# Two edits of the DMA order in a four-layer attention kernel: halves for the late query loads, later stores of x

## The chip, the cores and the metric

The kernel runs on one core of one Trainium2 chip. The metric is the device time of one execution in microseconds (us), taken as the median of several runs. Times inside the kernel come from one execution recorded by the hardware profiler; they count from the first instruction of the program (the span's start).

## The reference

Four layers of attention, one after the other; layers 0 and 2 use weights A, layers 1 and 3 weights B. Each has 32 query heads of 16 dimensions, and a single key head and value head for all of them. The sequence has 2048 rows of 512 numbers, in 32-bit floating point.

```python
def _A_ref(x, wq, wk, wv, wo):          # _B_ref is the same
    B, S, D = x.shape                   # 1, 2048, 512
    H = 32
    Dh = D // H                         # 16
    q = (x @ wq).reshape(B, S, H, Dh).transpose(0, 2, 1, 3)
    k = x @ wk
    v = x @ wv
    scores = jnp.einsum("bhqd,bkd->bhqk", q, k) * (Dh ** -0.5)
    p = _softmax(scores, axis=-1)
    o = jnp.einsum("bhqk,bkd->bhqd", p, v)
    return o.transpose(0, 2, 1, 3).reshape(B, S, H * Dh) @ wo

x = A_x
x = x + _A_ref(_layernorm(x, axis=-1), A_wq, A_wk, A_wv, A_wo)
x = x + _B_ref(_layernorm(x, axis=-1), B_wq, B_wk, B_wv, B_wo)
x = x + _A_ref(_layernorm(x, axis=-1), A_wq, A_wk, A_wv, A_wo)
x = x + _B_ref(_layernorm(x, axis=-1), B_wq, B_wk, B_wv, B_wo)
```

There are 4 layers x 32 heads x 2048 x 2048 = 537 million scores, and each needs an exponential.

## The kernel before

**Units of work.** The queries of a layer come in 4 blocks `b` of 512 rows, and the heads in 4 groups `m` of 8. A pair (layer, block, group) is the unit whose queries are loaded together; there are 64 of them. A pair is worked off in halves: 64 keys by 4 of its 8 heads by 512 queries, which makes one tile of 128 x 1024 scores. A first matmul step (`score`, letter `S` in the order) writes such a tile `st` into PSUM, ScalarE (ACT) takes its exponential into one of 16 tiles `pt`, and TensorE (PE) multiplies `pt` with the values into `acc`. There are 4096 halves. 3658 of them take their exponential on ACT (line 868). The other 438 take it on VectorE (DVE), as a polynomial (lines 902 to 920): their scores go to the bank `by_v`, and `score_v` takes them `AHEAD` = 24 halves ahead of the one that `S` is at. Beside these run the products of the layer norm, keys, values, queries and outputs.

**What sets the order.** `ORDER` is a string of some 18,000 letters, worked out beforehand; each letter is one step on PE, ACT or DVE. The order of instructions on each compute engine is therefore fixed in the text. `Q` in that string calls `load_q`.

**Queries.** The queries of a pair are made on PE in 16 bits (`q_clamp`, `q_rest`), go out to a scratch tensor `qscr` (DMA `qs<-qs`, line 483), and come back by `load_q` in another layout as a tile `qt` of 128 partitions x 4 x 512 (512 KB, 4 KB a partition). The index of 4 counts two heads each: halves with `h` = 0 read `qt[:, 0:2]`, halves with `h` = 1 read `qt[:, 2:4]`. There are two `qt` buffers, so that a load can start when the scores of the pair before last have been made. Layer 0 goes over its first four pairs in four rounds of keys, and layers 1 to 3 over their first three pairs in two rounds, so that such a pair is loaded anew for each round: 85 loads in all.

**How a load is issued.** All these DMAs are issued by SyncE (SP), in program order on one queue; a DMA that has to wait holds up those behind it. `first_uses` works out from `ORDER` at which exponential each load is first used (`uses`). When that is `ROOM` = 20 or more exponentials away, `load_q` issues four quarters, three exponentials apart: the first at once, the others through the list `later`, which `issue_due` looks at after every exponential. `issue` makes such a DMA wait for the exponential before last:

```python
tc.add_manual_dep(d, exps[-2].name, ...)   # in issue(): exps[-1] is the one just written
```

59 loads go that way. When the first use is nearer, the whole 512 KB go as one DMA; that happens 26 times: 17 loads at the start of layer 0 (the first at 19.00 us, before the first exponential, the last at 232.80 us) and three each at 995 to 1025 us, 1841 to 1869 us and 2689 to 2716 us, where the next layer's first pairs begin. For the first the distance is 0, for the other 25 it is 5 to 7 exponentials, and in 21 of these the first reader is a `score_v` with `h` = 1.

**Residual.** `out_add` adds the attention's output to a tile of x (128 rows), and stores it to the scratch tensor `xscr` (DMA `xs<-xt`, line 510, 256 KB). It is loaded back a layer later (`xt<-xs`, line 398). There are 48 such stores.

Of the kernel before, what the change touches and what calls it, by code (L numbers as in the profile page):

```python
# [25 lines left out]
BQ = S // NB  # L26
# [8 lines left out]
ROOM = 20  # L35
# [233 lines left out]
def fast_path(ctx, tc, x_in, weights, out, flag):  # L269
    nc = tc.nc  # L270
    PE, V, A, G, SP = nc.tensor, nc.vector, nc.scalar, nc.gpsimd, nc.sync
# [13 lines left out]
    def need(*key):  # L285
        assert key in done, key
# [34 lines left out]
    xscr = [scr.tile([P, D], F32, name=f"xs{t}") for t in range(NT)]  # L321
# [177 lines left out]
    def out_add(l, t, ps):  # L499
        x = xt[l, t]  # L500
        V.scalar_tensor_tensor(x, ps, 1 / VS / WS, x, ALU.mult, ALU.add)
        del xt[l, t]
        if (l, t) == (NL - 1, NT - 1):
            for h, eng in enumerate((SP, A)):
                h = slice(64 * h, 64 * h + 64)
                eng.dma_start(out[t * P:(t + 1) * P, :][h], x[h])
        elif l == NL - 1:
            SP.dma_start(out[t * P:(t + 1) * P, :], x)
        else:
            SP.dma_start(xscr[t], x)  # L510
            xt[l + 1, t] = x


# [149 lines left out]
    def add_outputs(l, b, after):  # L663
        for t in range(4 * b, 4 * b + 4):
            def prods(t=t):
                c = slice((t - 4 * b) * P, (t - 4 * b + 1) * P)
                ps = []
                for m in range(NM):
                    ps += three([p[:, c] for p in ot[l, b, m]], [p[:, m] for p in wt["wo", l]])
                return ps  # L670

            add_product(prods, after, ("o", l, b))
            work.add_dve("oa", lambda t=t: out_add(l, t, beside), key=("end",))
        work.add_dve("od", lambda: done.add(("o", l, b)), key=("od", l, b))
# [77 lines left out]
    for l in range(NL):  # L752
        first = 16 * l
        n, cuts = (4, [0, 4, 8, 12, NK]) if l == 0 else (3, [0, 12, NK])
# [19 lines left out]
    exps, later, loads = [], [], [0]  # L774

    def first_uses():

        n, v, some, count, open_ = 0, -1, set(), 0, False
        nth = [sum(k <= g for k in to_load) - 1 for g in range(len(groups))]
        uses = {}  # L780
        for what in ORDER:
            if what == "S":
                while n in some:
                    n += 1
                uses.setdefault(nth[halves[n][0]], count)
                n += 1
                count += 1
            for w in STEPS[what] if what in STEPS and what != "S" else "":
                if w in "VW":
                    if not open_:  # L790
                        while n in some:
                            n += 1
                        v = max(v + 1, n + (AHEAD if n < len(halves) - LATE else NEAR))
                        some.add(v)
                        uses.setdefault(nth[halves[v][0]], count)
                    open_ = not open_
        return uses

    uses = first_uses()
# [7 lines left out]
    def spaced(dmas, apart):  # L807

        for k, dma in enumerate(dmas):
            if k == 0 or apart == 0:  # L810
                dma()
            else:
                later.append((len(exps) + k * apart, dma))
        later.sort(key=lambda t: t[0])
# [6 lines left out]
    def load_q():  # L821
        g = to_load.popleft()
        l, b, m = pairs[groups[g][0]]
        need("q", l, b, m)
        t = qt[groups[g][0]] = qop.tile([P, 4, BQ], F16, name="qt")
        q = qscr[l % 2][b][m].rearrange("r t d h q -> (r t d) (h q)")
        k = loads[0]
        loads[0] += 1
        if uses[k] - len(exps) < ROOM:
            SP.dma_start(t, q.unsqueeze(1).to_broadcast([64, 2, 4 * BQ]))  # L830
            return

        def part(h):
            return SP.dma_start(t[:, h], q[:, h * BQ:(h + 1) * BQ].unsqueeze(1).to_broadcast([64, 2, BQ]))

        spaced([lambda h=h: part(h) for h in range(4)], 3)

    def moving(n, r):
        g, c, h = halves[n]
# [227 lines left out]
    def finish():  # L1067
# [43 lines left out]
        products(1, last)  # L1111
        products(3, first)
        out_add(l, 4 * b, banks[0])
        times(cs[2])
        invert(cs[3])
        rest(cs[2])
        products(2, last)
        out_add(l, 4 * b + 1, banks[1])
        times(cs[3])
        out_add(l, 4 * b + 2, banks[2])  # L1120
# [12 lines left out]
    with tc.manual_schedule():  # L1133
# [95 lines left out]
        for c in (0, 1):  # L1229
            part(c, others, scaled(stat[key, c]))  # L1230
        q_rest(0, 0, 0, ps, (SP, A))
        load_q()
        kps = st[1][:, 0:512]
        for c in range(NC):
# [24 lines left out]
    with tc.manual_schedule():  # L1259
        on_pe = [what for what in ORDER if what in STEPS or what in "FP"]  # L1260
        for what in ORDER:
            if what in on_pe[:1]:
                on_pe.pop(0)
            if what == "S":
                score()
            elif what in STEPS:
                step(what, on_pe[0] if on_pe else "S")
            elif what == "F":
                whole()
            elif what == "Y":  # L1270
                touch()
            elif what == "P":
                work.next_pe().whole()
            elif what == "X":
                work.step_dve()
            elif what == "I":
                exp_first()
            elif what in "01":
                chain("01".index(what))
            elif what == "G":  # L1280
                evacs.popleft()()
            elif what == "D":
                divs.popleft()()
            elif what == "Q":
                load_q()
            else:
                raise ValueError(what)
# [158 lines left out]
```

## Time and profile before

| | before |
|---|---|
| time, median of 3 runs | 3426.78 us (3426.61 to 3429.51) |
| the profiled execution's own time | 3429.39 us |
| its span, first to last instruction | 3427.6 us |
| TensorE clock granted | 0.999 |
| PE busy | 3360.2 us (98%), 97703 matmuls and as many weight loads |
| ACT busy | 3382.2 us (99%); the 3658 exponentials 3367.7 us |
| DVE busy | 3253.7 us (95%) |
| GpSimd busy | 134.1 us (4%) |
| DMA | 147.81 MB, 43 GB/s in the mean |

Three engines are busy nearly all the time, so the lost time is small and has to be looked for in single places: an idle stretch of ACT, what PE did then, and what the DMA queues moved. Exponentials overlap each other (one takes 1102 ns in the mean, and one starts every 925 ns), so that ACT shows as idle only after the previous one has ended. In the timeline a bracket such as [0.74 <-issue] means that the engine was idle for 0.74 us before the row and that nothing the profile shows ended the wait; SPq rows are DMA issues of SP, and `x2` merges two rows. In the table by stretches, the columns are the busy time of each engine with its number of instructions, the granted clock, the busy share of the 16 DMA engines and GB/s.

### The profile page before, as it was taken

The numbers are of one execution on the slowest core, as the hardware profiler recorded it, in microseconds if no ns is written. First come the engines' busy times: TensorE is split into PE (matmuls) and PEld (weight loads), VectorE is DVE, ScalarE is ACT, GpSimd is POOL, SyncE is SP. The second block draws the span as 40 slices with busy tenths as digits, with TensorE's granted clock in tenths as the row PEclk, the third lists the DMA queues.
The fourth block names the chain that finished last, engine by engine and source line by source line (L and its number), as shares of the span: only waits on it lengthen the run. The fifth ranks groups of instructions, "written<-read, shape, count | busy, mean of one in ns | idle before, by whom it ended". The sixth has DMA issues, their size and how long they took to land.

```text
span 3427.6 us, 206561 instructions
## 1 busy us (share of the span) xinstructions
PE 3360.2 (98%) x97703; PEld 2087.5 (61%) x97703; DVE 3253.7 (95%) x4436; ACT 3382.2 (99%) x3688; POOL 134.1 (4%) x137
## 2 busy tenths in 40 slices
PE   9999999999999999999999999999999999999998
PEld 5666566555566666646556666664646666554554
DVE  7889999999989999999998999999999899999998
ACT  8999999999999999999999999999999999999997
POOL 3000000000000000000000000000000000000000
PEclk9999999999999999999999999999999999999999
DMA  3121111011012111101012211110101211111010
GB/s 114 59 81 47 32 43 45 28 36 39 30 54 54 50 50 37 41 25 44 21 31 58 57 49 37 42 43 24 46 19 37 67 46 37 36 49 29 22 42 21
DMA packets 119316, 147.81 MB, mean 43 GB/s; under 512 B 32889, under 2 KB 81017, under 8 KB 118457
## 3 DMA queue, kind: packets, MB, share of 16 engines
q1 hardware_dynamic: 116888, 133.65, 13.5%
q8 instruction: 765, 12.53, 1.5%
q10 hardware_dynamic: 1568, 0.85, 0.1%
q14 instruction: 95, 0.77, 0.1%
HBM read 90.57 MB, written 34.59 MB: 37 GB/s over the span
## 4 chain that ended last, share of the span: by engine, by line
PE 62%; ACT 27%; DVE 8%; issue 2%; DMA 0%; DVEq 0%; ACTq 0%
PE acc L532 32%; ACT pt L868 27%; PE st L532 16%; PE beside L532 10%; PE by_v L532 2%; DVE pt L902 1%; DVE poly L919 1%; PE beside L426 1%; DVE pt L913 1%; DVE poly L920 1%; DVE mant L916 1%; DVE pt L918 1%; PE beside L569 0%; DVE sum L1017 0%; DVE vop L462 0%
## 5 line engine op out<-in xcount | busy, mean ns | idle before, releaser
L868 ACT ACTIVATE pt<-st 128x1024 f32<-128x1024 f32 x3658 | 3367.7, 1102 | 20.6 <-PE st L532 17.6
L532 PE MATMUL acc<-pt,vop 64*32 64x256 f32 (+1 forms) x51728 | 2893.8, 434 | 4.5 <-issue 2.1
L532 PE MATMUL st<-qt,kop 64*32 64x512 f16 x29264 | 1763.2, 380 | 48.7 <-ACT pt L868 25.1
L532 PEld LDWEIGHTS acc<-pt,vop 64*32 64x32 f32 x51728 | 1331.2, 106 | 253.5 <-DVE sum L1017 12.0
L532 PEld LDWEIGHTS <-kop 64*32 64x32 f16 x32768 | 797.2, 90 | 922.3 <-issue 642.6
L902 DVE TENSOR_SCALAR pt<-by_v 128x512 int32<-128x512 f32 x876 | 598.9, 684 | 36.2 <-PE by_v L532 31.1
L913 DVE SCALAR_TENSOR_TENSOR pt<-poly,pt 128x1024 f32<-128x1024 f32 x438 | 536.2, 1224 | 3.3
L920 DVE SCALAR_TENSOR_TENSOR poly<-poly,mant 128x1024 f32<-128x1024 f32 x438 | 535.6, 1224 | 3.1
L919 DVE SCALAR_TENSOR_TENSOR poly<-mant 128x1024 f32<-128x1024 f32 x438 | 534.5, 1221 | 0.0
L532 PE MATMUL beside<-xnT,wq 64*32 64x512 f16 x5760 | 438.8, 376 | 1.5 <-issue 0.6
L532 PE MATMUL beside<-wo,ot 64*32 64x512 f16 x5472 | 406.4, 376 | 0.5 <-DVE gqk L497 0.3
L532 PE MATMUL by_v<-qt,kop 64*32 64x512 f16 x3504 | 350.1, 376 | 1.8 <-DVE pt L902 1.3
L918 DVE TENSOR_SCALAR pt<-pt 128x1024 int32<-128x1024 int32 x438 | 304.8, 696 | 4.6
L916 DVE TENSOR_SCALAR mant<-pt 128x1024 int32<-128x1024 int32 x438 | 301.8, 690 | 6.3
L532 PEld LDWEIGHTS <-wq 64*32 64x32 f16 x5760 | 170.5, 92 | 49.7 <-issue 12.8
L532 PEld LDWEIGHTS <-ot 64*32 64x32 f16 x5472 | 158.6, 92 | 39.7 <-issue 4.9
L477 POOL TENSOR_TENSOR sq<-qs 128x512 bf16<-128x512 f16 x64 | 73.6, 1151 | 873.6 <-DVE qs L474 873.6
L532 PE MATMUL beside<-xnT,wkv 64*32 64x512 f16 x1344 | 97.5, 376 | 0.0
L1017 DVE COPY sum<-acc 128x512 f32<-128x512 f32 x126 | 84.1, 687 | 11.9 <-PE acc L532 8.3
L413 POOL TENSOR_TENSOR rstd<-var,nhalf 128x4 f32<-128x4 f32 x15 | 21.7, 1446 | 1451.0 <-DVE var L412 1451.0
L474 DVE TENSOR_SCALAR qs<-beside 128x512 f16<-128x512 f32 x62 | 42.7, 689 | 16.9 <-PE beside L532 9.5
L998 DVE COPY seen<-beside 128x1 f32<-128x1 f32 x92 | 14.3, 156 | 41.2 <-PE beside L532 34.2
(133 smaller groups left out, 833.5 us busy)
## 6 DMA issues: line engine op xcount, KB each, us to landing
qt<-qs SPq DMA_DIRECT2D x236, 128.0 KB
qs<-qs SPq DMA_DIRECT2D x127, 128.0 KB
rec<-rs SPq DMA_DIRECT2D x63, 256.0 KB
qt<-qs SPq DMA_DIRECT2D x26, 512.0 KB
xs<-xt SPq DMA_DIRECT2D x48, 256.0 KB
xt<-xs SPq DMA_DIRECT2D x48, 256.0 KB
sum<-sum SPq DMA_DIRECT2D x252, 32.0 KB
xt<-in_A_x_dram SPq DMA_DIRECT2D x30, 256.0 KB
```

The costliest lines, as they stand in the source:

```text
L426: PE.transpose(ps[:, c * P:(c + 1) * P], xn[:, c * P:(c + 1) * P], ident)
L474: V.tensor_scalar(qs[:, 0], ps, BIG, -BIG, ALU.min, ALU.max)
L477: G.tensor_tensor(sq, qs[:, 0], qs[:, 0], ALU.mult)
L532: PE.matmul(o[32 * j:32 * j + 32], w[j][h], x[j][h], start=start, stop=stop, skip_group_check=True, tile_position=(64 * r, 32 * j))
L868: e = A.activation(pts[:, i], st[s], AF.Exp, scale=SCALE / UP / UP).ins
L902: w = V.tensor_scalar(e[:, 512 * r:512 * r + 512], by_v, SCALE / UP / UP * LOG2E * 2.0 ** 23, LEAD, ALU.mult, ALU.add).ins
L913: writer[i] = V.scalar_tensor_tensor(p, poly, C0, p, ALU.add, ALU.mult).ins
L916: lambda: V.tensor_scalar(mant.bitcast(I32), e, 0x3FFFFF, 0x3F800000, ALU.bitwise_and, ALU.bitwise_or),
L918: lambda: V.tensor_scalar(e, e, 0x7FC00000, HALVES, ALU.bitwise_and, ALU.bitwise_or),
L919: lambda: V.scalar_tensor_tensor(poly, mant, C2, mant, ALU.add, ALU.mult),
L920: lambda: V.scalar_tensor_tensor(poly, poly, C1, mant, ALU.add, ALU.mult),
L1017: V.tensor_copy(sums[pr, odd], acc[odd])
```

## The change

The first edit is in `out_add`: the store of x isn't issued at once, but put on the list `later` with a due number two exponentials on. The second is in `load_q`: a near load goes as two DMAs of 256 KB (`n` = 2: heads' index 0:2 and 2:4, 2 KB a partition each) instead of one of 512 KB. The first half is issued at once. The second is put on `later` one exponential on (`apart` = 1), so that it waits for the end of the exponential that was written last before the load; for the first load (`k` = 0), `apart` is 0 and both halves are issued one after the other. The quarters of the far loads stay as they are.

```diff
@@ out_add
         else:
-            SP.dma_start(xscr[t], x)
+            later.append((len(exps) + 2, lambda: SP.dma_start(xscr[t], x)))
             xt[l + 1, t] = x
@@ load_q
-        if uses[k] - len(exps) < ROOM:
-            SP.dma_start(t, q.unsqueeze(1).to_broadcast([64, 2, 4 * BQ]))
-            return
+        n = 1 if uses[k] - len(exps) >= ROOM else 2
 
         def part(h):
-            return SP.dma_start(t[:, h], q[:, h * BQ:(h + 1) * BQ].unsqueeze(1).to_broadcast([64, 2, BQ]))
-
-        spaced([lambda h=h: part(h) for h in range(4)], 3)
+            return SP.dma_start(t[:, h:h + n],
+                                q[:, h * BQ:(h + n) * BQ].unsqueeze(1).to_broadcast([64, 2, n * BQ]))
+
+        spaced([lambda h=h: part(h) for h in range(0, 4, n)], 3 if n == 1 else k > 0)
```

The instructions of PE, ACT, DVE and GpSimd stand in the same order as before; only SP's queue changes. All query loads now have line 832, the stores keep 510, and lines further down are one less.

SP around the three loads at 995 to 1025 us, before (`qt<-qs` is a query load with partitions and elements, `qs<-qs` the store of new queries, `den`, `rs`, `sum` and `rec` the chain that divides by the softmax's sums):

```order
L483 DMA qs_1_0_141<-qs 64x2x512 x2
L830 DMA qt<-qs_0_1_138 128x1x2048
L830 DMA qt<-qs_0_2_139 128x1x2048
L483 DMA qs_1_1_142<-qs 64x2x512 x2
L1025 DMA den<-sum_22417 64x1x32
L1025 DMA den<-sum_22452 64x1x32
L483 DMA qs_1_2_143<-qs 64x2x512 x2
L830 DMA qt<-qs_0_3_140 128x1x2048
L1048 DMA rs_169<-den 4x16x32 x2
```

Each load was one DMA there, and the next rows of the queue stood right behind it. SP at the same place now:

```order
L483 DMA qs_1_0_141<-qs 64x2x512 x2
L832 DMA qt<-qs_0_1_138 128x1x1024 x2
L832 DMA qt<-qs_0_2_139 128x1x1024 x2
L483 DMA qs_1_1_142<-qs 64x2x512 x2
L1024 DMA den<-sum_22433 64x1x32
L1024 DMA den<-sum_22468 64x1x32
L483 DMA qs_1_2_143<-qs 64x2x512 x2
L832 DMA qt<-qs_0_3_140 128x1x1024 x2
L1047 DMA rs_169<-den 4x16x32 x2
```

Each is two DMAs of half the size; what stood behind a load now stands behind its second half, which waits for an exponential.

SP around a store of x that comes between quarters of a load (the one at 569.77 us), before:

```order
L510 DMA xs_158<-xt 128x512
L834 DMA qt<-qs_2_3_132 128x1x512 x3
L510 DMA xs_159<-xt 128x512
L834 DMA qt<-qs_2_3_132 128x1x512
L1025 DMA den<-sum_14323 64x1x32
L1025 DMA den<-sum_14343 64x1x32
L510 DMA xs_160<-xt 128x512
```

And now:

```order
L510 DMA xs_158<-xt 128x512
L832 DMA qt<-qs_2_3_132 128x1x512 x4
L1024 DMA den<-sum_14339 64x1x32
L1024 DMA den<-sum_14359 64x1x32
L510 DMA xs_159<-xt 128x512
L510 DMA xs_160<-xt 128x512
```

The middle store went behind the last quarter and two small DMAs. `later` is a queue in which a new entry stands behind what is there already, so a store that is put on it while quarters are waiting goes out only behind them. 8 of the 48 stores change their place in the queue; the other 40 keep it, and wait for an exponential there.

## The prediction

> **What bounds the kernel now.** I read the page first (busy shares, the groups), then ACT's idle time in stretches behind each kind of DMA that the change touches, then the timeline at the worst of these.
>
> ```profile
> PE 3360.2 (98%) x97703; PEld 2087.5 (61%) x97703; DVE 3253.7 (95%) x4436; ACT 3382.2 (99%) x3688; POOL 134.1 (4%) x137
> q8 instruction: 765, 12.53, 1.5%
> L868 ACT ACTIVATE pt<-st 128x1024 f32<-128x1024 f32 x3658 | 3367.7, 1102 | 20.6 <-PE st L532 17.6
> ```
>
> PE and ACT run in lockstep, both full. ACT's exponentials have only 20.6 us of idle time in all, and 17.6 us of that are waits for scores from PE. A change of DMAs alone, with every engine's order kept, can win little more than this, so the question is which of these 20.6 us lie behind the DMAs that change. I asked for the stretch from 3 to 10 us after each issue, for line 868 alone: 24 near loads (without the first two), 59 far loads (from their first quarter) and 48 stores of x.
>
> ```profile
> 998.60:1005.60 7.00, 6.07 (x8) 1.00 0.06 19
> 1011.67:1018.67 7.00, 7.00 (x9) 1.00 0.19 40
> 1027.53:1034.53 7.00, 6.18 (x7) 1.00 0.28 76
> 2718.87:2725.87 7.00, 5.97 (x8) 1.00 0.42 139
> ...
> sum 168.00, ACT 163.12; mean ACT 6.80
> sum 413.00, ACT 411.17; mean ACT 6.97
> sum 336.00, ACT 335.31; mean ACT 6.99
> ```
>
> The three sums are near loads, far loads, stores. Behind near loads ACT idles 168.00 - 163.12 = 4.88 us, or 0.20 us a load; behind far ones 1.83/59 = 0.03 us; behind stores 0.69/48 = 0.014 us. The rows above the sums show that near loads differ: the one at 1008.67 us cost nothing, the one at 995.60 us 0.93 us. So I looked at that one.
>
> ```profile
> 993.96 1.55 SPq L483 DMA_DIRECT2D qs<-qs  x2
> 995.60 0.56 SPq L830 DMA_DIRECT2D qt<-qs  x1
> 1001.51 0.40 PE L532 MATMUL acc<-pt,vop 64*32 64x256 f32 x2 [0.74 <-issue]
> 1002.39 1.02 ACT L868 ACTIVATE pt<-st 128x1024 f32<-128x1024 f32 x1 [0.88 <-PE st L532]
> q1 hardware_dynamic: 431, 0.79, 77.8%
> q8 instruction: 1, 0.02, 5.7%
> ```
>
> PE stood still for 0.74 us and waited for no semaphore ("issue"), long after the load's data had come. The last two rows are the DMA view of 995.20 to 999.15 us and of 999.15 to 1000.20 us. In the first there is only data, on 77.8% of the engines' time; in the second, once the data has drained, one packet of queue 8, of instructions. The page counts 765 such packets; 97703 + 97703 instructions of PE over 765 make 255 each. So I read queue 8 as PE's own program, 256 instructions a packet, at one packet every 3427.6/765 = 4.5 us. My reading: the fetch was asked for while 128 KB + 128 KB + 512 KB were on the way, came only when they had drained, and PE ran out of instructions. The same sign, ACT idle for scores some 6 to 8 us after a near load, stands at eight other places:
>
> ```profile
> 113.86 1.02 ACT L868 ACTIVATE pt<-st 128x1024 f32<-128x1024 f32 x1 [0.31 <-PE st L532]
> 154.99 1.94 ACT L868 ACTIVATE pt<-st 128x1024 f32<-128x1024 f32 x2 [0.36 <-PE st L532]
> 184.15 1.02 ACT L868 ACTIVATE pt<-st 128x1024 f32<-128x1024 f32 x1 [0.41 <-PE st L532]
> 1031.89 1.02 ACT L868 ACTIVATE pt<-st 128x1024 f32<-128x1024 f32 x1 [0.82 <-PE by_v L532]
> 1875.88 1.02 ACT L868 ACTIVATE pt<-st 128x1024 f32<-128x1024 f32 x1 [0.33 <-PE st L532]
> 2696.02 1.97 ACT L868 ACTIVATE pt<-st 128x1024 f32<-128x1024 f32 x2 [0.22 <-PE st L532]
> 2709.51 1.03 ACT L868 ACTIVATE pt<-st 128x1024 f32<-128x1024 f32 x1 [0.31 <-PE st L532]
> 2722.35 0.39 PE L532 MATMUL st<-qt,kop 64*32 64x512 f16 x3 [0.90 <-issue]
> 2722.79 1.02 ACT L868 ACTIVATE pt<-st 128x1024 f32<-128x1024 f32 x1 [1.03 <-PE st L532]
> ```
>
> These follow the loads at 106.87, 148.73, 177.07, 1024.53, 1868.73, 2689.00, 2701.63 and 2715.87 us; with the one at 995.60 us there are nine.
>
> **The change, part by part.**
>
> *Near loads, the stalls that can go.* The gain is bounded above by near loads behaving as far ones: 4.88 - 24 x 0.03 = 4.1 us of idle. A stalled exponential also loses its overlap with the one before (1.10 us long, one every 3427.6/3658 = 0.94 us), 0.17 us at nine places = 1.5 us. Together 5.6 us; the lower bound is 0, if the fetch waits for both halves as it did for the whole. I take 5.6 us, because a load alone already has both results: behind the one at 1008.67 us, not preceded by stores, nothing was lost. [...]
>
> *Near loads, the second half.* It is issued later by the wait for an exponential. How much later, and for whom, shows at a quiet load:
>
> ```profile
> 1008.67 0.55 SPq L830 DMA_DIRECT2D qt<-qs  x1
> 1013.05 0.40 PE L532 MATMUL by_v<-qt,kop 64*32 64x512 f16 x4
> 249.59 0.54 SPq L834 DMA_DIRECT2D qt<-qs  x1
> 250.80:251.80 1.00, 1.00 (x2) 1.00 0.39 131
> 1010.00:1011.55 1.55, 1.55 (x2) 1.00 0.95 338
> 22.35:22.73 0.38, 0.00 (x0) 1.00 0.00 0
> ```
>
> The first reader of a near load is mostly DVE's share, on `by_v`, and that reads the second half: here 4.38 us after the issue. The 512 KB moved from 1.33 to 2.88 us after the issue (1010.00:1011.55), and a quarter of a far load issued at 249.59 us took 1.0 us (250.80:251.80). Half a load I estimate between these, 1.2 us. The buffer comes free when PE has made the last score of an older pair; the exponential of that score, for which the second half waits, ends about one exponential later, so I take 1.15 us. Then the data runs from 1.15 + 1.33 = 2.5 to 3.7 us. From the last data to the first matmul, the first load shows 0.38 us (the last row: DMA idle from 22.35 us, PE starts at 22.73 us). That makes 4.1 us against 4.38: in time, by 0.3 us. Where a fetch steps in between the halves, the second half's part on that DMA engine is pushed back by the fetch's 0.96 us (5.7% of 16 engines in 1.05 us). It ends then some 0.4 us too late. This bears on those of the nine loads whose second half is read first; in three (177.07, 995.60, 2689.00 us) it is the first half, and the one at 2715.87 us has its reader 6.5 us on, so five remain: 5 x 0.4 = 2.0 us lost. The remaining loads cost nothing by this sum; if the data takes the 1.55 us of a whole load, 4.45 us against 4.38 is a wait of 0.1 us at 15 of them, 1.5 us. Range of this term: 0 to 3.5 us lost; I take 2.0.
>
> *The first load.*
>
> ```profile
> 22.73 0.63 PE L532 MATMUL st<-qt,kop 64*32 64x512 f16 x16 [1.02 <-DVE gv L469]
> 23.21 1.03 ACT L868 ACTIVATE pt<-st 128x1024 f32<-128x1024 f32 x1 [3.54 <-PE st L532]
> ```
>
> PE waits 1.02 us for it before the first exponential (DVE, whom the row names, isn't what the code waits for here: the matmul needs `qt`). With two halves the first score can start when the first half has landed, about 1 us earlier, but PE then meets the second half, which is issued 0.57 us later (one more issue on SP) and lands when the whole did. PE gains little, ACT one exponential's start. Between 0 and 1.0 us; I take 0.4, since both are full from there on.
>
> *Stores of x.* They land 2 exponentials later, some 1 to 2 us; nobody reads them for hundreds of us. Behind all 48 there were 0.69 us of idle time, so -0.7 us is the most that can be won. Eight now stand right behind quarters of a load: 256 KB after 128 KB, again a pile for a fetch to wait behind. At the price of the smallest stall above (0.31 us and the lost overlap) for all eight that is +3.8 us; I take 0, as their length together is less than the 768 KB of the case at 995.60 us, and the stall needs a fetch at that very moment.
>
> *SP and the queue.* 26 DMAs more, at 0.55 us each, cost SP 14 us spread over 26 places. SP has no other work than issues and their waits; behind a near load stand stores of new queries and the division's small DMAs, which go out 1 to 1.7 us later. DVE waited for `rec` in no more than
>
> ```profile
> DVE sum L1065 <- DMA rec<-rs: 1.3, 2, 0.9
> ```
>
> so that chain has slack nearly everywhere. I cost it at nothing; if its cover were gone at the five loads that are followed by it, 5 x 1 us.
>
> *Sum.* -5.6 (stalls) + 2.0 (late halves) - 0.4 (first load) + 0 (stores, SP) = -4.0 us, from the profiled execution's 3429.39 us to 3425.4 us. That execution is 2.6 us above the median of 3426.78 us, close to the slowest of the three; I carry the difference over to the median: 3422.8 us, 0.12% less.
>
> **Rivals.**
>
> *Nothing moves.* The fetch still waits for both halves. For it: where stores precede a load (995.60 us), SP reaches the second half late, so that it may follow the first without a break; 128 + 128 + 256 + 256 KB are then one pile as before. Against it: a wait for an exponential stands between, and in most places it is over 1 us. Time: 3426.8 - 0.4 = 3426.4 us. [...]
>
> *Late halves take over: slower.* The second half lands after its reader is there. It needs a landing later than 4.4 us after the first issue; by my sum it is at 4.1 us. Each 0.1 us beyond costs 21 loads 2.1 us. If a half takes as long as the whole now (1.55 us) and waits for a fetch (0.96 us) everywhere, it lands at 5.4 us: 21 x 1.0 = 21 us minus the 6.0 us of gains, 3442 us. It is slower than now from 0.3 us of lateness at every load. Against it: 512 KB take only 1.55 us today.
>
> *All is won.* No half is late, the first load gives 1.0 us, the one bad store 0.7 us: -7.3 us, 3419.5 us.
>
> *Stores collide.* The eight stores cost 3.8 us, the rest goes as forecast: 3426.6 us.
>
> **How the numbers follow.** A measurement of this kernel tells some 0.2% (6.9 us) from no change, so "faster" is below 3419.9 us and "slower" above 3433.6 us. Forecast (part of the stalls gone, 3419.9 to 3425.5 us): 0.52, nearly all inside 0.2%. 3425.5 to 3430 us together: 0.24, of which nothing moves 0.14, stores collide 0.05, and gains that late halves eat up 0.05. All is won, below 3419.9 us: 0.16. Late halves cost more than 0.1% net: 0.08, of which beyond 3433.6 us: 0.06. That gives faster 0.16, same 0.78, slower 0.06. The range leaves out the worst of late halves and the best of "all is won": 3417.5 to 3429.5 us.
>
> **What the next profile would show.** Right: the idle sum behind near loads falls from 4.88 us to about 2, PE's waits on "issue" behind them go, and the instruction packet after 995.6 us starts before 998.5 us instead of 999.15. Wrong: PE rows on `by_v` with idle time at each load (late halves), or "issue" rows at the same places (nothing moves). Idle behind the eight moved stores would show the last rival. I would be wrong most plainly if the nine stalls came from something other than the pile of data, or if they depend on the execution: the 2.6 us between the profiled run and the median may be some of these very stalls.

## The result, and the profile after

| | before | after |
|---|---|---|
| median | 3427.0 us (6 runs, 3423.57 to 3429.51) | 3447.45 us (6 runs, 3445.71 to 3449.76) |
| profiled execution | 3429.39 us | 3449.76 us |

The ratio is 1.006, with a 95% interval of 1.0047 to 1.0073: 20 us slower (16 to 25), where 4 us faster was forecast, outside the range of 3417.5 to 3429.5 us.

The first lines are the page of the changed kernel, engines and two groups (busy us, mean ns of one, idle us before them and what ended most of it); the last two are from its list of who waited for whom (us in total, times, longest).

```profile
PE 3361.2 (97%) x97703; PEld 2085.1 (60%) x97703; DVE 3253.3 (94%) x4436; ACT 3384.0 (98%) x3688; POOL 134.0 (4%) x137
L867 ACT ACTIVATE pt<-st 128x1024 f32<-128x1024 f32 x3658 | 3369.5, 1102 | 38.8 <-PE st L532 35.0
L532 PE MATMUL by_v<-qt,kop 64*32 64x512 f16 x3504 | 350.2, 378 | 20.9 <-DMA qt<-qs 18.9
ACT pt L867 <- PE st L532: 35.0, 43, 9.1
PE by_v L532 <- DMA qt<-qs: 18.9, 12, 7.8
```

ACT's idle time before exponentials rose from 20.6 to 38.8 us; their busy time hardly changed (3367.7 and 3369.5 us). The new row is the last: PE now waits at `by_v` for the query DMA, 12 times and 18.9 us in all, near the 20 us of the loss. Before, that group had 1.8 us of idle time and none of it for the query DMA. The table by stretches puts it to single loads (3 to 10 us after the first half's issue, 24 near loads as in the prediction):

```profile
216.67:223.67 7.00, 5.47 (x6) 1.00 0.12 35
1008.88:1015.88 7.00, 6.10 (x8) 1.00 0.05 17
2731.66:2738.66 7.00, 2.89 (x4) 0.98 0.36 82
...
sum 168.00, ACT 154.75; mean ACT 6.45
```

ACT idles 168.00 - 154.75 = 13.25 us behind these loads, against 4.88 us before. The worst is the load at 2728.66 us. Its timeline (start, duration, engine, line; in brackets the idle time and what ended it):

```profile
2728.66 0.55 SPq L832 DMA_DIRECT2D qt<-qs  x1
2729.26 2.44 SPq L483 DMA_DIRECT2D qs<-qs  x2
2731.82 1.20 SPq L1047 DMA_DIRECT2D rs<-den  x2
2733.07 2.87 SPq L1050 DMA_DIRECT2D sum<-sum  x4
2736.39 0.68 SPq L1054 DMA_DIRECT2D rec<-rs  x1
2737.17 0.59 SPq L832 DMA_DIRECT2D qt<-qs  x1
2741.17 0.62 PE L532 MATMUL by_v<-qt,kop 64*32 64x512 f16 x4 [7.83 <-DMA qt<-qs]
2743.62 1.02 ACT L867 ACTIVATE pt<-st 128x1024 f32<-128x1024 f32 x1 [9.06 <-PE st L532]
```

Between the two halves SP issued nine other DMAs: two stores of new queries, and the division's two `rs`, four `sum` and one `rec`, some of which wait themselves. The second half went out 8.51 us after the first, not one exponential. PE, whose next instruction reads that half, stood for 7.83 us, and ACT for 9.06. The reason is in how `later` works: an entry is written into SP's program when the next exponential is written, and everything that the order puts ahead of that exponential stands ahead of it in the queue. The same at the second load of all:

```profile
25.11 0.55 SPq L832 DMA_DIRECT2D qt<-qs  x1
25.71 2.01 SPq L398 DMA_DIRECT2D xt<-in_A_x_dram  x4
27.76 0.56 SPq L832 DMA_DIRECT2D qt<-qs  x1
33.18 0.62 PE L532 MATMUL by_v<-qt,kop 64*32 64x512 f16 x4 [3.30 <-DMA qt<-qs]
34.33 1.02 ACT L867 ACTIVATE pt<-st 128x1024 f32<-128x1024 f32 x1 [3.81 <-PE st L532]
```

Here four loads of x, 1 MB, are in between. The last 2 KB packet of these and of the two halves ended at 32.78 us, 5.02 us after the second half's issue, and PE started 0.40 us after that. Two more loads (1867.46 and 2713.75 us) had their second half 1.96 and 1.97 us after the first, behind stores of queries. I compared the start of each exponential in the two traces, near load by near load: behind these four, exponentials are later by 5.74, 1.34, 0.69 and 8.77 us, together 16.5 us of the 20.4 by which the profiled executions differ.

At the first and the last of these the lateness is more than PE's wait (5.74 us behind a wait of 3.30 us; 8.77 us behind one of 7.83 us, although a stall that had cost 1.17 us at this place is gone). In both, the granted clock fell while PE stood (at 31.63 and 2738.40 us) and came back 5.27 and 4.05 us after PE had gone on, at 38.45 and 2745.22 us (the columns are those of the table by stretches, for PE alone):

```profile
31.63:38.45 6.82, 5.27 (x64) 0.50 0.17 57
2738.40:2745.22 6.82, 4.05 (x72) 0.50 0.20 65
```

PE worked for 5.27 and 4.05 us at a clock of 0.50, and the rows on `by_v` at 33.18 and 2741.17 us took 0.62 us, where the row at 219.78 us below took 0.40. At half the clock I estimate that as 2.6 and 2.0 us lost on top of the waits. In the kernel before, the clock is at 0.50 only at the program's end, from 3423.19 us on, behind the last exponential (3406.80 us). How long a stall must be for this isn't shown: behind PE's wait of 1.60 us at 219.78 us the clock stayed at 1.00.

At the other near loads the second half went out 0.64 to 1.34 us after the first. At a quiet one that cost nothing:

```profile
99.70 1.65 SPq L832 DMA_DIRECT2D qt<-qs  x2
104.37 0.39 PE L532 MATMUL by_v<-qt,kop 64*32 64x512 f16 x4
```

Both halves are merged in the first row; the reader started without idle time. Eight others lost 0.2 to 1.6 us of PE's time each. The worst of these, with two answers of the DMA view between the timeline's rows (216.70 to 216.85 us and 218.24 to 219.30 us; packets, MB, share of 16 engines):

```profile
213.67 1.60 SPq L832 DMA_DIRECT2D qt<-qs  x2
q8 instruction: 1, 0.02, 61.6%
q1 hardware_dynamic: 8, 0.01, 6.6%
219.78 0.40 PE L532 MATMUL by_v<-qt,kop 64*32 64x512 f16 x4 [1.60 <-DMA qt<-qs]
220.87 1.97 ACT L867 ACTIVATE pt<-st 128x1024 f32<-128x1024 f32 x2 [1.53 <-PE st L532]
```

A packet of PE's instructions started at 216.79 us, while the second half was moving, and took 1.48 us. The half's last seven packets came only then, one behind the other, at 218.25 to 219.30 us. All its others were done at 217.9 us.

### The profile page after: what moved, and what is told of

Read it like the earlier page. It is cut to its first block, busy times and chain, and to the rows that moved or that the text cites. A ratio compares the mean times of both kernels' runs of the same rounds, so it can differ in the third digit from the quotient of the medians.

```text
span 3448.0 us, 206606 instructions
## 1 busy us (share of the span) xinstructions
PE 3361.2 (97%) x97703; PEld 2085.1 (60%) x97703; DVE 3253.3 (94%) x4436; ACT 3384.0 (98%) x3688; POOL 134.0 (4%) x137
## 3 DMA queue, kind: packets, MB, share of 16 engines
q1 hardware_dynamic: 120632, 133.66, 13.4%
## 4 chain that ended last, share of the span: by engine, by line
PE 56%; ACT 31%; DVE 8%; DMA 2%; issue 2%; SPq 1%; DVEq 0%; ACTq 0%
ACT pt L867 31%; PE acc L532 29%; PE st L532 15%; PE beside L532 9%; PE by_v L532 2%; DMA qt<-qs 2%; DVE pt L901 1%; DVE poly L918 1%; DVE poly L919 1%; PE beside L426 1%; DVE pt L912 1%; DVE mant L915 1%; DVE pt L917 1%; PE beside L569 0%; SPq L1050 0%
## 5 line engine op out<-in xcount | busy, mean ns | idle before, releaser
L867 ACT ACTIVATE pt<-st 128x1024 f32<-128x1024 f32 x3658 | 3369.5, 1102 | 38.8 <-PE st L532 35.0
L532 PE MATMUL by_v<-qt,kop 64*32 64x512 f16 x3504 | 350.2, 378 | 20.9 <-DMA qt<-qs 18.9
```

What stands on the lines that cost most here:

```text
L532: PE.matmul(o[32 * j:32 * j + 32], w[j][h], x[j][h], start=start, stop=stop, skip_group_check=True, tile_position=(64 * r, 32 * j))
L867: e = A.activation(pts[:, i], st[s], AF.Exp, scale=SCALE / UP / UP).ins
```

## Experiments

Each experiment is told against the runs of the kernel before that ran beside it, on the same chip. There are two theories. By the first, the loss is the lateness of the second half, above all where SP's queue lets something in between. By the rival, it is spread over all loads, or lies in the stores.

**The two edits apart.** First the change of `load_q` alone, stores of x at once:

```diff
-            later.append((len(exps) + 2, lambda: SP.dma_start(xscr[t], x)))
+            SP.dma_start(xscr[t], x)
```

> The near loads in halves, the stores of x as before. Theory (the second halves come late: at four places other DMAs stand before them in SP's queue, at others they wait for an exponential and a fetch): all of the loss is here, 3447 us (3444 to 3450), +20 us. Rival (the later stores of x do it, by blocking SP or by piling up on other data): near the time before, 3422 to 3428 us.

Measured: 3448.38 us, ratio 1.0064 (1.0048 to 1.0079), PE's wait for the query DMA 20.2 us. Then the stores alone, `load_q` as before:

> The stores of x two exponentials later, the near loads whole as before. Theory: no difference, 3427 us (3424 to 3429). Rival (the stores do it): 3440 to 3447 us.

Measured: 3425.68 us beside 3426.03, ratio 1.0001 (0.9992 to 1.001). The whole loss is in the loads; the stores move nothing that five rounds can tell.

**Both halves at once.** `apart` is 0 for all near loads, stores as after the change:

```diff
-        spaced([...], 3 if n == 1 else k > 0)
+        spaced([...], 3 if n == 1 else 0)
```

> As the changed kernel, but every near load issues its two halves one right after the other, with nothing between. Theory of the late second half: the loss goes, 3422 to 3428 us; PE's waits for qt (18.9 us before by_v in the changed kernel) fall below 3 us. If in addition a fetch of instructions can pass between two halves that are both queued, 3422 to 3424 us, if it can't 3427 us. Rival (it is the smaller pieces themselves, more DMAs and 2 KB lines instead of 4 KB, that are slow): stays at 3440 to 3447 us.

Measured: 3427.12 us beside 3426.03, ratio 1.0003 (0.9994 to 1.0012). A row of the list of waits, and the sum of the stretches:

```profile
PE by_v L532 <- DMA qt<-qs: 3.2, 3, 1.7
sum 168.00, ACT 163.74; mean ACT 6.82
```

The loss is gone, so it came from the wait between the halves and not from there being two DMAs; PE's waits, 3.2 us, stay a little above the 3 us expected. But nothing is won either: 168.00 - 163.74 = 4.26 us of ACT are idle, against 4.88. Two of the nine loads of the prediction (148.73 and 1024.53 us) lost another 0.8 and 0.7 us, five (177.07, 995.60, 2689.00, 2701.63 and 2715.87 us) won 0.5 to 0.8 us. So a fetch does get in earlier even when both halves are queued: behind the loads at 177.07, 2689.00 and 2701.63 us its packet started 2.6 to 2.9 us after the issue, against 3.3 to 4.3 us in the kernel before. At the two that lost, the packet held up the half that PE was waiting for (waits of 1.22 and 1.67 us).

**Only the four loads between whose halves something stood.** At these, and at the first, both halves go at once; the other 21 keep their exponential:

```diff
-        spaced([...], 3 if n == 1 else k > 0)
+        spaced([...], 3 if n == 1 else k not in (0, 1, 52, 71, 72))
```

> The changed kernel, but at four near loads (the 2nd, the 53rd, the 72nd and the 73rd of the 85) both halves are issued one behind the other, as at the first load. At these four the trace of the changed kernel has other DMAs or a chain of waits between the halves: four loads of x of 256 KB at the 2nd, stores of new queries at the 53rd, stores and the small DMAs of the division at the 73rd. The other 21 loads keep one exponential between the halves.
> Theory 1 (most of the loss is that something else gets in between on SP's queue): the exponentials behind these four loads started later by 5.7, 1.3, 0.7 and 8.8 us than before the change, 16.5 us of the 20.4. So about 16 us come back: 3428 to 3433 us, PE's waits on by_v for the query DMA fall from 18.9 us to 5 to 7 us, none longer than 1.7 us. What is left is one exponential of lateness and a fetch, in sum about +5 us less the stalls that go.
> Theory 2 (every half that goes out one exponential later is late, whatever stands between): 21 of 25 loads stay late, so no more than a fifth of the loss comes back: above 3440 us.

Measured: 3428.6 us beside 3425.44, ratio 1.0012 (1.0003 to 1.0021).

```profile
PE by_v L532 <- DMA qt<-qs: 5.1, 6, 1.6
```

As theory 1 had it: four of 25 loads hold some 17 of the 20 us (a loss of 20.5 us for the changed kernel and of 3.2 us here, each against the kernel before that ran beside it), near the 16.5 us of their places. What is left, 3 us, fits the lateness by one exponential and a fetch at the other loads, but no run takes the two apart. The profiled execution, the slowest of its kind with 3432.95 us, also had 3.41 us at a clock of 0.50 (44.90 to 48.31 us) behind a wait of 1.56 us.

**One load alone.** The kernel before, with the load at 2715.87 us in halves and all others whole:

```diff
+            if k != 72:
                 SP.dma_start(t, q.unsqueeze(1).to_broadcast([64, 2, 4 * BQ]))
+            else:
+                spaced([... one DMA for h = 0:2, one for h = 2:4 ...], 1)
```

> The kernel before, with one load alone changed: the 73rd of the 85 (the last near one) goes in two halves, the second one exponential later, as in the changed kernel. All others stay whole.
> Theory 1 (SP's queue lets other DMAs and their waits in between the halves, and PE stands until the second half has come): the exponentials behind this one load are later by 8.8 us as in the trace of the changed kernel, less nothing: 3433 to 3436 us beside about 3426, with one wait of PE on by_v for the query DMA of 7 to 8 us; the chain that divides comes first.
> Theory 2 (the 7.8 us there are what 20 us of earlier lateness add up to, shifting the division's chain against the load): with the rest as before the halves are a microsecond apart as elsewhere, and the loss at this load is 0 to 1 us: 3425 to 3427 us.

Measured: 3433.1 us beside 3423.53, ratio 1.0023 (1.0013 to 1.0034), 4 to 12 us. A row of the list of waits, then the timeline at that load:

```profile
PE by_v L532 <- DMA qt<-qs: 7.2, 2, 7.0
2716.40 0.56 SPq L833 DMA_DIRECT2D qt<-qs  x1
2724.27 0.59 SPq L833 DMA_DIRECT2D qt<-qs  x1
2728.09 0.61 PE L532 MATMUL by_v<-qt,kop 64*32 64x512 f16 x4 [7.01 <-DMA qt<-qs]
```

One load of 85 makes the exponentials behind it 8.06 us later, where those ahead of it are only 0.5 us late (12.8 us in the changed kernel): its halves are 7.87 us apart in an otherwise unchanged kernel. Here too the clock was at 0.50 for 6.8 us (2725.53 to 2732.35 us). Theory 2 of this run falls.

**The needed half first.** `first_uses` also notes which half (`h`) the first reader of each load reads. That half is issued at once, the other one exponential later; stores as after the change.

```diff
+        hs = range(4) if n == 1 else (2 * side[k], 2 - 2 * side[k])
-        spaced([lambda h=h: part(h) for h in range(0, 4, n)], 3 if n == 1 else k > 0)
+        spaced([lambda h=h: part(h) for h in hs], 3 if n == 1 else k > 0)
```

> As the changed kernel, but each near load issues first the half that is read first, and the other one exponential later (it is read some 13 us later). Theory: no load is late any more, and fetches of instructions find a gap: 3421 us (3418 to 3424), PE's waits for qt under 1 us. Rival (the pieces or the waits of SP cost time by themselves): 3435 us or more.

Measured: 3423.38 us beside 3426.03, ratio 0.9992 (0.9983 to 1.0001). The stretches' sum, and the load that cost 8.8 us above:

```profile
2710.88 0.55 SPq L835 DMA_DIRECT2D qt<-qs  x1
2717.87 0.59 SPq L835 DMA_DIRECT2D qt<-qs  x1
2716.23 0.39 PE L532 MATMUL by_v<-qt,kop 64*32 64x512 f16 x2
...
sum 168.00, ACT 166.74; mean ACT 6.95
```

The other half goes out 6.99 us later here too, behind the same DMAs. PE doesn't wait for it: it read what it needed at 2716.23 us, before the other half was issued. ACT's idle time behind near loads falls from 4.88 to 1.26 us, and no wait of `by_v` for the query DMA is left. This is the gain that the prediction counted on, at about half its size (2.65 of 5.6 us in the medians), and five rounds can't quite tell it from no change.

**The other half four exponentials later.** The same with `4 * (k > 0)` instead of `k > 0`, and stores of x at once:

> The needed half first, as in the run with that name, but the other half goes four exponentials later instead of one, and the stores of x go out at once as before the change. Theory (an instruction fetch waits behind the pile of data in front of it, so what is asked for sooner than needed should be spread as far as the reader allows): the same stalls gone as with one exponential (3423.4 us, no waits of by_v for a query DMA) and the rest of them too, 3420 to 3424 us. Rival (with the needed half first the pile is small enough and nothing more can be won; or the other half now comes late for its own reader, 6.5 us on): 3423 to 3428 us, with waits of PE on st for the query DMA in the rows.

Measured: 3422.49 us beside 3425.44, ratio 0.9992 (0.9983 to 1.0001), idle 168.00 - 166.89 = 1.11 us. The time is in the theory's range, but what the later half wins over the run before can't be told from nothing: 2.95 against 2.65 us under the kernel before, 1.11 against 1.26 us of idle time.

**First load whole.** As the run before, with the first load as one DMA:

> The needed half first and the other one four exponentials later, and the first load of all whole, as before the change (its halves made PE wait twice: the exponentials behind it were 0.4 to 0.9 us later in every run with halves). Stores of x at once. Theory: 0.5 us better than with the first load in halves, 3421 to 3423 us, and about 0.1% under the kernel before, at the edge of what five rounds can tell. Rival (what is saved at single loads is given back elsewhere, as the sums of single places and the medians differ by 1 to 2 us): 3424 to 3427 us.

Measured: 3419.72 us beside 3423.53, ratio 0.999 (0.9981 to 0.9999).

```profile
sum 168.00, ACT 166.28; mean ACT 6.93
```

1.72 us of idle time are left of the 4.88, no less than in the two runs before it (1.26 and 1.11 us). It is faster than the kernel before by 0.1%, just resolved, and by 0.7% than the changed one (0.999 against 1.006, both to the kernel before). The median lies below the 3421 us expected, but the kernel before was faster beside it too (3423.53 against 3425.44 us). Neither the medians nor the stretches show that the first load's part of it is 0.5 us.

**Where do the nine stalls come from?** The kernel before with 64 more matmuls in the warm-up, so that every later instruction of PE stands 128 places further on. If PE stalls where a packet of 256 instructions ends behind a load, the stalls must move; if the load itself causes them, they stay.

```diff
-        for i in range(24):
+        for i in range(24 + 64):
```

> The kernel before with 64 more matmuls of the warm-up ahead of all work, so that all later instructions of PE stand 128 places further on and the places where a packet of 256 instructions ends move by half a packet. Nothing else is changed.
> Theory 1 (PE stalls where its next packet of instructions was asked for behind a load): the stalls change their places. Those behind the loads at 148.73, 177.07, 1024.53, 1868.73 and 2689.00 us (times of before; the end of a packet lay 1.25 to 1.54 us behind the issue of the load and now lies 0.4 to 0.6 us ahead of it) are gone, and new ones of 0.3 to 0.9 us of ACT stand behind the loads issued at 134.76 and 163.19 us, where none was (ends of packets now 1.35 to 1.38 us behind the issue).
> Theory 2 (the stall comes from the load itself, the port of its tile or its length): the same nine places as before, 0.2 to 1.0 us each, and none behind those two.
> The time as before plus some us for the longer warm-up, under both.

Measured: 3428.48 us, one execution. The stretches behind the loads that before were issued at 148.73, 163.19, 177.07, 1024.53, 1855.20, 1868.73 and 2689.00 us, with the sum over 24, and the timeline behind the fifth (issued at 1860.11 us now):

```profile
156.58:163.58 7.00, 6.84 (x9) 1.00 0.04 9
170.78:177.78 7.00, 6.66 (x9) 1.00 0.18 42
185.09:192.09 7.00, 7.00 (x9) 1.00 0.45 114
1033.13:1040.13 7.00, 6.97 (x9) 1.00 0.28 85
1863.11:1870.11 7.00, 5.83 (x7) 1.00 0.19 66
1878.03:1885.03 7.00, 7.00 (x9) 1.00 0.32 88
2694.74:2701.74 7.00, 7.00 (x9) 1.00 0.06 19
...
sum 168.00, ACT 164.84; mean ACT 6.87
1860.11 0.55 SPq L830 DMA_DIRECT2D qt<-qs  x1
1866.43 0.41 PE L532 MATMUL st<-qt,kop 64*32 64x512 f16 x7 [0.79 <-issue]
```

Of the five that should go, four fell from 0.41, 0.82, 0.33 and 0.22 us to 0.00 to 0.03, and the fifth (148.73 us) from 0.36 to 0.16. Of the two that should come, one did (163.19 us: 0.00 before, 0.34 now), the other did not (134.76 us: 0.00). A large one came at 1855.20 us, 1.17 us, where none had been; there the end of a packet had moved to 0.87 us behind the issue. Part of this comes without a shift: in two executions with whole loads and PE's program in its old place (the stores alone, and one load alone) the stalls at 1868.73 and 2689.00 us were at 0.00 to 0.17 us as well. The load at 1024.53 us is clear of that (0.71 to 0.93 us in the three executions without the shift, 0.03 with it), and so are the one at 995.60 us (0.81 to 0.93, now 0.05) and the two new ones (0.00 in all three). So the place of a stall goes with PE's instruction packets and not with the load, as far as one execution shows it. Which of the ends that lie behind a load cause one isn't settled by their distance alone.

## Why the prediction was wrong

*The step that failed is the term "Near loads, the second half", +2.0 us (0 to 3.5).* It rested on "the exponential [...] for which the second half waits, ends about one exponential later, so I take 1.15 us" for every load. That holds for 21 of 25 (0.64 to 1.34 us). For the other four the second half went out 1.96 to 8.51 us later, for two reasons: a DMA that waits holds up those behind it (the store of queries at 2729.26 us stood for 1.78 us, the next one, at 2731.10 us, for 0.61), which the front part says, and an entry of `later` is written into the queue after all that the order puts ahead of the next exponential, which neither the front part nor the prediction says. I looked at SP's order at three loads, where the halves stood together, and took them for all. At the load at 2728.66 us the order shows the nine DMAs in between before anything runs. Measured, PE's twelve waits for the second half are 18.9 us in place of the 2.0: 13.4 us at these four loads (3.30 + 1.10 + 1.18 + 7.83) and 5.5 us at the eight others. The clock of 0.50 behind the two longest comes on top; the working had no term for it.

*The late part behind a fetch* was forecast for five loads at 0.4 us (its own figures give 0.6: 4.1 + 0.96 against 4.38); it came at eight, with 0.2 to 1.6 us. The packet's length, taken at 0.96 us, was right for seven of them (0.88 to 1.02 us); the eighth, at 216.79 us, took 1.48. And it isn't only the loads that stalled before: in all eight a packet of instructions started while the halves' data moved, also at 43.47, 71.65, 213.67, 1019.06 and 1852.77 us, loads that weren't among the nine.

*SP and the queue, 0.* The working asked what stands behind a near load and goes out later. That cost nothing: with the needed half first, the same DMAs stand in the queue and nobody waits. What stands in front of the second half was not asked.

*Stalls that can go, -5.6.* The cause was right for most of the nine, the amount not. Behind eight of the loads the packet of instructions started 2.1 to 3.3 us after PE had reached number 193 of a block of 256 instructions, against 0.83 us in the median (the last section has both the count and the median). The stall at 113.86 us isn't of this kind: its packet started after 0.93 us, and ACT's idle time there is 0.30 or 0.31 us in ten of the eleven profiles, with whole loads and with halves (0.20 us in the shifted kernel). Its cause stays open. In the changed kernel two of the nine loads, at 177.07 and 2689.00 us, gained, 0.56 and 0.51 us; their first reader reads the first half. At the load that was at 995.60 us and is at 1005.88 us now, nothing moved in this execution, as the rival of that name said. The DMA view from its issue to 1009.53 us and from there to 1010.50 us, and the timeline behind it:

```profile
q1 hardware_dynamic: 556, 0.77, 72.5%
q8 instruction: 1, 0.02, 6.2%
1011.91 0.40 PE L532 MATMUL acc<-pt,vop 64*32 64x256 f32 x2 [0.70 <-issue]
```

The halves went 0.64 us apart, so their data made one pile as before, the fetch came at its end, 3.65 us after the issue (3.56 before; the sign asked for was less than 2.9), and PE stood 0.70 us where it had stood 0.74. In three other runs with halves at this load (the loads alone, both halves at once, the four loads not overtaken) they also went 0.62 to 0.65 us apart, but the packet started 3.20, 3.01 and 2.94 us after the issue and ACT idled for 0.38, 0.32 and 0.29 us instead of 0.90. So the changed kernel's profile shows the worst of four, and halves did help here elsewhere.

With both halves at once, the packet behind this load, which started 3.01 us after the issue, took 0.96 us, the data paused from 3.45 us on, and the rest of the second half moved from 3.96 us on. There the fetch came ahead of the second half's end, in the changed kernel, at 3.65 us, behind it; what decides between the two isn't shown.

In the kernel before, PE stood without a semaphore for over 0.1 us at only ten of the 763 places with number 193 (the last section says how they are counted). Five of the ten belong to the nine stalls.

With the needed half first and the first load whole, 3.2 of the 4.88 us of idle time went, and the time fell by 3.8 us: the -5.6 was within reach at some two thirds, by another edit.

*The first load, -0.4.*

```profile
22.36 0.41 PE L532 MATMUL st<-qt,kop 64*32 64x512 f16 x8 [0.36 <-DMA qt<-qs]
22.83 2.17 ACT L867 ACTIVATE pt<-st 128x1024 f32<-128x1024 f32 x2 [2.89 <-PE st L532]
23.50 0.41 PE L532 MATMUL st<-qt,kop 64*32 64x512 f16 x8 [0.73 <-DMA qt<-qs]
```

The first exponential came 0.38 us earlier (22.83 against 23.21), as forecast. But PE then waited 0.73 us for the second half, and the fifth exponential was 0.55 us later than before; 0.30 us of that is the load's own issue (19.30 against 19.00 us). In the five other runs with the first load in halves the fifth exponential lies 0.25 us earlier to 0.16 us later than before, and in the three with the first load whole (the shifted kernel left out) 0.26 us earlier to 0.08 us later. So the term is nothing that these runs can tell, and not -0.4.

*Stores, 0:* right (ratio 1.0001). *The rivals:* the outcome belongs to "late halves take over", which had a chance of 0.08 and was priced as an even lateness at 21 loads. Its sum of 21 us is near the 20 measured, but by another distribution: the mean lateness is small, and one load alone costs more than all that could be won. The price should have been asked at the worst load, not at the quiet one.

The doubt whether the stalls depend on the execution was partly right: in the run of the stores alone, with whole loads, ACT idles 3.42 us behind the 24 loads (168.00 - 164.58). The load at 995.60 us shows 0.90 us again, the one at 2715.87 us 0.10 instead of 1.03.

## What to carry to other kernels

A DMA that is put off "by one exponential" is put off by everything that the program writes into the same queue before that exponential, with all its waits (here nine DMAs and 8.51 us); go through the queue's order at each place, and cost the worst one. When a load is split, look first at which part is read first: issued first, that part makes the other one's lateness free, here even 6.99 us of it. Parts that follow each other within a microsecond let a fetch in earlier at most of the places looked at here (2.6 to 2.9 us after the issue behind three loads, against 3.3 to 4.3 us), but the fetch then delays the later part (waits of 1.22 and 1.67 us at two others): that part should be the one that is read last. And look at the granted clock behind a long stall: here it was at 0.50 for 6.8 us behind two of them, which I estimate above at 2.6 and 2.0 us on top of their length.

## What the hardware showed

- In both kernels queue 8 moved 765 packets of 16 KB, one for every 255 matmuls and weight loads of PE; I take them for PE's program. PE's rows of the trace were counted in order of their start, from 0, in blocks of 256. All ten places of the kernel before where PE stood for over 0.1 us and waited for no semaphore, and all five of the changed one, have number 193, which the text above calls the end of a packet (1001.51 us in the kernel before, 1011.91 us in the changed one, 1866.43 us in the shifted one). In the kernel before, one packet started in 750 of the 762 stretches from one number 193 to the next, 0.83 us after the stretch's start in the median. In the stretch ahead of the ten it started 2.1 to 3.7 us after; ahead of 1011.91 us in the changed kernel 2.6 us (1006.94 to 1009.53 us), ahead of 1866.43 us in the shifted one 3.3 us (1860.97 to 1864.25). PE went on 1.25 to 1.50 us after that packet had come; 1.41 and 1.25 us at these two, having stood for 0.70 and 0.79 us.
- A packet of instructions of 1.48 us lay ahead of a half's last seven packets: the half, 256 KB, was complete at 219.30 us, 1.4 us later than all its other packets (217.9 us).
- In the changed kernel 8.51 us between two halves cost PE 7.83 us; with the order of the halves exchanged 6.99 us cost none.
- Behind PE's waits of 3.30 and 7.83 us the granted clock was at 0.50 for 6.8 us each, 5.27 and 4.05 us of them with PE at work; behind one of 1.56 us it was at 0.50 for 3.41 us (in the run with the four loads not overtaken), and behind one of 1.60 us it stayed at 1.00.
